# A planned kernel re-planned: new priorities and costs, VectorE and GpSimd kept apart in the plan, 30 unread matmuls behind the last output

## The chip, the cores and the metric

One core of a Trainium2 chip runs the whole problem. The metric is the device time in microseconds (us) of one execution; three executions of the kernel before gave 342.11, 342.50 and 342.98 us, median 342.5 us.

## The reference, cut to what matters

The problem is an attention block with quadratic features, followed by a gated feed-forward block with a spatial gate. Batch 4, 4 heads, sequence 1088, head width 32, model width 128, feed-forward width 1024.

```python
def phi(x):                       # 8 x 8 products of two projections of each row
    a = einsum('rd,bhsd->bhsr', S1, x); b = einsum('rd,bhsd->bhsr', S2, x)
    return einsum('bhsi,bhsj->bhsij', a, b).reshape(..., 64)
q_p, k_p = phi(q), phi(k)
kv, z = einsum('bhsf,bhsd->bhfd', k_p, v), sum(k_p, axis=2)
x = (q_p @ kv) / (q_p @ z + 1e-6)            # heads side by side: [4, 1088, 128]

h = gelu_tanh(x @ w_in)                      # [4, 1088, 1024]
u, v = h[..., :512], h[..., 512:]
v_n = (v - mean(v)) / sqrt(var(v) + 1e-6) * g_ln
v_s = einsum('ts,bsd->btd', w_sg, v_n) + b_sg[None, :, None]   # 1088 x 1088 along the sequence
out = x + (u * v_s) @ w_out
```

The product with `w_sg` (1088 by 1088, for each of 4 batches and 512 channels) is most of the arithmetic.

## The kernel before, in words

TensorE holds a float32 number as a sum of two float32r words (`_h` and `_l`), and a product of two such numbers is three float32r matmuls: high by high, low by high, high by low. VectorE and ScalarE make the words: ScalarE copies a tile into float32r (the high word), VectorE subtracts it from the tile (the low word). A few small products (features of k, sums over k, a transposition, the last output) stay in float32, and each of their matmuls stands as two instructions in the trace.

The sequence is cut into nine tiles of 128 rows, the outputs of the spatial product into three column blocks `CH` of 362, 362 and 364. Batch 0 runs first: attention (functions ending in `_0`), then the normalised gate tiles, then the spatial product, in which lines 744, 746 and 748 are the three kinds of matmul of `z0` and lines 1248, 1250 and 1252 those of the next block of channels. The matrix `w_sg` comes in as float32, ScalarE makes its high words (`w_h`, line 717), and GpSimd makes most of its low words (`w_l`, line 761, function `w_lo`, 21 pieces); the last two tiles go to VectorE (`late_low`, line 768). The words of a gate tile are made at lines 722 and 723 (function `part`). For batches 1 to 3 a scheme with fewer products runs (function `pair`), which needs combinations of `w_sg` that `combine` makes (lines 945 to 955) and sends through DRAM. While one batch runs, `attention(b)` prepares the next (lines 983 and 991 are its k products, 1010 the low words of q, 1031 and 1033 its feature products, 1073 to 1075 the gate half of the first layer).

Nothing in the text of the program sets the order of the work. Each step is a task given to `Plan.add` with its engine, a duration that the author supplies, the keys it reads and writes, and the buffers it takes and frees. `Plan.order` then plays all engines forward: it gives each TensorE task a due time from its position `pos`, works due times back through the dependencies, and at every moment picks the task that can start first, the earlier due time ahead. The resulting sequence is written out engine by engine, so that each engine runs its instructions in exactly this order, and one that waits holds up all behind it. Positions come from tables (`HEAD`, `SIDE`, `UNITS`, `OUTS`). The supplied durations are functions of the column count:

```python
dv = lambda n: 0.075 + n * 1.04e-3     # VectorE
ac = lambda n: 0.09 + n * 0.83e-3      # ScalarE
pe = lambda n: 0.005 + n * 0.443e-3    # TensorE
```

In this plan VectorE and GpSimd never hold one another up. A piece of `w_lo` is planned at 0.92 us, and the seven steps of `split64` (the float64 weights turned into float32, lines 512 to 518) at 0.42 to 0.67 us each for 512 columns.

At the start 14 matmuls whose result nobody reads run on TensorE (line 315). At the end, `finish` (lines 1185 to 1195) makes the last output block in two halves: two VectorE steps, float32 matmuls of 182 columns (line 1191), an addition on VectorE, and one DMA for each half, on SyncE's and on ScalarE's queue.

Of the kernel before, what the change touches and what calls it, by code (L numbers as in the profile page):

```python
# [18 lines left out]
P = 128  # L19
# [22 lines left out]
HEAD = [  # L42
# [5 lines left out]
]  # L48
SIDE = [
    dict(  # L50
        k=[-66.1568, -83.0896, -64.9264, -188.0582, -81.0397, -187.723, -70.4624, -77.7272, -77.1695],
        m=[-5466.7093, -5528.8972, -5437.2895, -5515.3945, -5393.6818, -5437.3893, -5432.8724, -5431.1056, -5501.4403],
        q=[634.6912, 673.1882, 647.6791],
        n=[64.1725, 20.8317, 52.3833, 22.0789, 61.9314, 20.9482],
        v=[11.3231, 63.8001, 41.2931, 152.8686, 24.7648, 29.2218, 100.774, 74.9017, 33.0816],
    ),
    dict(
        k=[104.6639, 64.2414, 66.2022, 93.2106, 94.9278, 59.1733, 77.7462, 87.1414, 48.0262],
        m=[68.9081, 117.0063, 70.3394, 41.7758, 72.8224, 116.9436, 126.4316, 41.681, 63.3969],
        q=[852.2799, 861.6072, 861.644],  # L60
        n=[161.3675, 69.9811, 170.238, 131.9103, 210.1209, 170.0751],
        v=[254.1817, 359.0423, 298.7528, 265.5773, 271.6818, 346.4955, 246.9949, 378.9035, 373.6698],
    ),
    dict(
        k=[445.2317, 1445.0667, 347.8146, 1453.4091, 1437.2462, 338.8656, 338.4801, 305.2576, 1462.8265],
        m=[240.7848, 278.0785, 215.5893, 305.508, 281.8525, 193.6687, 261.5745, 239.3695, 222.0321],
        q=[50.5261, 76.0513, 90.6998],
        n=[9375.8047, 9362.4456, 9374.739, 9361.4134, 9375.5758, 9369.7237],
        v=[127.1668, 148.5901, 276.214, 166.0724, 146.6282, 183.2742, 285.7286, 189.6866, 298.3922],
    ),  # L70
]
UNITS = [
    [41.9793, 27.5684, 38.7608],
    [147.9841, 100.1362, 157.0333],
    [169.7846, 137.9183, 129.767],
    [-33.9611, -31.7642, 487.2107],
    [631.6264, 620.4938, 639.6873],
    [1176.1661, 1190.4829, 1174.4149],
    [1286.0986, 1285.4686, 1259.311],
    [1120.4627, 1088.6707, 1101.0447],  # L80
    [174.8899, 174.1921, 174.7564],
    [53.0992, 83.7767, 45.9969],
    [176.2013, 188.4403, 182.9185],
    [151.0717, 161.8047, 172.948],
    [2273.7069, 2316.3133, 2263.2321],
    [5199.6257, 5107.2826, 5108.796],
    [40.0875, 25.0253, 23.3802],
    [1191.973, 1191.1916, 1192.4143],
]
OUTS = [  # L90
    [-0.3445, 11.4454, -11.4747],
    [202.992, 203.0658, 205.4131],
    [-9.1239, -4.2989, 47.4457],
    [638.4281, 736.5059, 730.313],
    [432.0253, 382.0212, 436.7813],
    [-22.0562, -0.7362, -25.8101],
    [565.5554, 575.2591, 561.2372],
    [-23.4218, 22.1653, -28.2736],
    [-23.1409, -8.8413, 1.757],
    [69.2499, -36.941, -43.6304],  # L100
    [3.6224, 443.7439, 439.3914],
    [1520.0977, 1533.1464, 1521.1808],
    [2020.1792, 1998.4613, 2022.0916],
    [-33.5198, -32.7719, -44.5421],
    [217.0347, 211.7791, 208.6139],
    [-45.2017, -46.2515, 4.5],
]
# [18 lines left out]
class Plan:  # L126
# [5 lines left out]
    def __init__(self, units):  # L132
        self.tasks, self.units, self.got = [], units, {}
        self.wrote, self.read = {}, {}

    def add(self, eng, dur, f, r=(), w=(), take=(), free=(), pos=None, late=None, start=None, after=(), kb=0):
        n = len(self.tasks)
        take = dict(take)
# [14 lines left out]
        self.tasks.append(dict(eng=eng, dur=dur, f=f, deps=deps, take=take, free=list(free), pos=pos, late=late, start=start, kb=kb))  # L153
# [6 lines left out]
    def order(self, free, t0):  # L160
# [20 lines left out]
        self.got, seq = {}, []  # L181
        clock = dict(free)
# [25 lines left out]
        while len(seq) < total:  # L208
            for e in stale:
                best[e] = None  # L210
                for i in can[e]:
                    x = max(clock[e], ready[i])
                    for k in T[i]["take"].values():
                        if not units[k]:
                            break
                        x = max(x, units[k][0][0])
                    else:
                        if best[e] is None or (x, last[i], i) < best[e]:
                            best[e] = x, last[i], i
# [11 lines left out]
            clock[e] = x + T[i]["dur"]  # L231
            if e == "SP" and T[i]["kb"]:
# [19 lines left out]
def tile_kernel(ctx: ExitStack, tc: tile.TileContext, qd, kd, vd, sd, wd, bd, wind, gd, woutd, identd, outd):  # L252
# [153 lines left out]
    pe = lambda n: 0.005 + n * 0.443e-3  # L406
# [33 lines left out]
    turns = iter(HEAD)  # L440

    def step(name, eng, dur, f, after=(), **kw):
        if eng == "PE":
            kw["pos"] = next(turns)
# [54 lines left out]
    def split64(name, hi, lo, raw, n, whole, after, last, by=V):  # L499
# [28 lines left out]
        step((name, "hi"), "A", 0.62, lambda: A.copy(hi, t()), [(name, 3)])  # L528
        step((name, "l1"), "V", 1.0, lambda: V.tensor_sub(t(), t(), f32(hi)), [(name, "hi"), (name, 5)])
        step((name, "l2"), "G" if by is G else "V", d[8] * 2.0, lambda: by.tensor_add(lo, t(), e()), [(name, "l1"), (name, 6)], w=last)  # L530
# [63 lines left out]
    for c in range(3):  # L594
        pk = ("pk0", c)
        step(pk, "PE", 0.68, lambda c=c: k1_0(c), ["sk", "k0" if c == 0 else "k1"], take={pk: "ps"})
        step(("kb0", c), "A", 0.25, lambda c=c: A.copy(kb0(c), ps(("pk0", c))[:, : 3 * P].rearrange("p (t c) -> p t c", t=3)[:, :, 32:64]), [pk])
        for i in range(3):
            t = 3 * c + i
            kk = [("vn", 2, t, x) for x in range(2)]  # L600
            step(("kp0", t), "V", 0.4, lambda c=c, i=i, t=t: features(vn[:, t, 512:768], ps(("pk0", c))[:, P * i : P * i + P], kb0(c)[:, i]),
# [43 lines left out]
    step("sabl", "G", 1.37, lambda: G.tensor_sub(sw[1], sab().rearrange("q x p c -> q (x p c)"), f32(sw[0])), ["sabh"])  # L645
# [702 lines left out]
```

## Time and profile before

| | us |
|---|---|
| median of three runs | 342.5 (342.11 to 342.98) |
| profiled execution, span from first to last instruction | 340.6 |
| the median less this span (what lies around the span) | 1.9 |
| TensorE busy | 327.8 (96%) |
| VectorE busy | 268.3 (79%) |
| ScalarE busy | 220.5 (65%) |
| GpSimd busy | 51.5 (15%) |

The profiled execution is told by its span; no other time of it is given, so the median stands beside it. A row of a timeline gives the start and the length of an instruction; matmuls are pipelined, so the distance of two starts is the time that one costs, and the length is about twice that. The bracket at the end of a timeline row is the idle time of the engine ahead of it, and who ended it. The 40 slices of the page are 8.5 us each.

### The profile page before, as it was taken

How to read it: one execution, taken by the hardware profiler on the slowest of the kernel's cores; microseconds unless marked ns; L12 is line 12 of the kernel's file. 1: busy time of each engine (PE TensorE's matmuls, PEld its weight loads, DVE VectorE, ACT ScalarE, POOL GpSimd, SP SyncE). 2: the span in 40 equal slices, each digit the busy share in tenths (PEclk: the TensorE clock that was granted, in tenths of full speed). 3: DMA queues.
4: the chain of work that ended last, by engine and by line, in shares of the span. 5: the costliest groups of instructions: out<-in, count | busy, mean ns of one | idle time of the engine just before them, and what ended most of it. 6: DMA issues, size and time to landing. Idle time of an engine off the chain costs nothing.

```text
span 340.6 us, 6042 instructions
## 1 busy us (share of the span) xinstructions
PE 327.8 (96%) x1988; PEld 319.1 (94%) x1988; DVE 268.3 (79%) x603; ACT 220.5 (65%) x533; POOL 51.5 (15%) x123
## 2 busy tenths in 40 slices
PE   8989869998999999999999999999999999999995
PEld 8987769998999989999998999999999999999994
DVE  4888999978976599999965699879854985786663
ACT  6689851376889975845669985487589834343330
POOL 1795681000003200000000600000021200000000
PEclk9999997999999999999999999999999999999999
DMA  7999174547746767999888356694569737384711
GB/s 241 371 398 334 36 201 120 133 114 195 186 146 192 197 184 229 276 275 312 265 262 246 111 167 206 177 311 146 174 179 283 241 102 247 104 269 117 237 41 65
DMA packets 56175, 68.87 MB, mean 202 GB/s; under 512 B 5008, under 2 KB 53456, under 8 KB 56144
## 3 DMA queue, kind: packets, MB, share of 16 engines
q1 hardware_dynamic: 56000, 68.40, 66.3%
q8 instruction: 15, 0.25, 0.3%
q14 instruction: 16, 0.13, 0.1%
q10 hardware_dynamic: 144, 0.09, 0.1%
HBM read 59.48 MB, written 8.99 MB: 201 GB/s over the span
## 4 chain that ended last, share of the span: by engine, by line
PE 83%; DVE 7%; DMA 6%; issue 1%; ACT 1%; SPq 0%; DVEq 0%
PE pz L892 15%; PE pz L894 15%; PE pz L893 15%; PE ps L807 2%; PE po L846 2%; PE ps L809 2%; PE ps L808 2%; PE po L845 2%; PE po L844 2%; PE ps L991 2%; PE pz L903 2%; PE pz L904 2%; DMA eb<-dq 2%; PE ps L1073 2%; PE ps L1075 2%; PE ps L1074 2%
## 5 line engine op out<-in xcount | busy, mean ns | idle before, releaser
L892 PE MATMUL pz<-w_h,ar 128*128 128x362 f32 (+1 forms) x288 | 96.1, 334 | 0.0
L894 PE MATMUL pz<-w_l,ar 128*128 128x362 f32 (+1 forms) x288 | 94.5, 328 | 0.0
L893 PE MATMUL pz<-w_h,ar 128*128 128x362 f32 (+1 forms) x288 | 94.3, 328 | 0.0
L892 PEld LDWEIGHTS pz<-w_h,ar 128*128 128x128 f32 x288 | 54.3, 188 | 0.5
L893 PEld LDWEIGHTS pz<-w_h,ar 128*128 128x128 f32 x288 | 54.3, 188 | 0.5
L894 PEld LDWEIGHTS pz<-w_l,ar 128*128 128x128 f32 x288 | 54.2, 188 | 0.0
L867 ACT CAST ar<-vn 128x512 fp32r<-128x512 f32 x40 | 24.5, 618 | 25.9 <-PE pz L894 25.1
L868 DVE TENSOR_TENSOR ar<-vn,ar 128x512 fp32r<-128x512 f32 x40 | 27.4, 686 | 13.4 <-ACT ar L867 13.0
L366 POOL TENSOR_TENSOR st<-st 128x4 f32<-128x4 f32 (+2 forms) x8 | 2.3, 285 | 189.5 <-DVE st L348 189.5
L838 ACT CAST gh<-gt 128x362 fp32r<-128x362 f32 (+1 forms) x47 | 23.0, 493 | 10.1 <-PE po L845 7.2
L813 ACT ACTIVATE u<-ps 128x362 f32<-128x362 f32 (+1 forms) x48 | 22.3, 471 | 10.9 <-DVE gt L837 6.5
L839 DVE TENSOR_TENSOR gl<-gt,gh 128x362 fp32r<-128x362 f32 (+1 forms) x47 | 24.7, 530 | 4.4 <-ACT gh L838 3.3
L383 ACT ACTIVATE vn<-vn,st 128x512 f32<-128x512 f32 x33 | 25.5, 811 | 0.6 <-POOL st L377 0.6
L837 DVE TENSOR_TENSOR gt<-gt,u 128x362 f32<-128x362 f32 (+1 forms) x47 | 24.6, 529 | 0.5 <-ACT u L813 0.2
L761 POOL TENSOR_TENSOR w_l<-w_f,w_h 128x362 fp32r<-128x362 f32 (+1 forms) x21 | 22.8, 1110 | 2.4 <-ACT w_h L717 2.1
L823 DVE SCALAR_TENSOR_TENSOR gt<-pz,g_col,b_bc 128x362 f32<-128x362 f32 (+1 forms) x31 | 18.1, 592 | 4.8 <-PE pz L894 3.4
L1085 ACT ACTIVATE kp<-vn,st 128x512 bf16<-128x512 f32 x27 | 19.5, 722 | 0.3
L1082 ACT ACTIVATE vn<-ps 128x512 f32<-128x512 f32 x27 | 16.0, 593 | 4.9 <-PE ps L1075 4.8
L991 PE MATMUL ps<-vx,kp 128*128 128x128 f32 x108 | 15.9, 275 | 0.7 <-DVE kp L320 0.7
L846 PE MATMUL po<-gl,wout_h 128*128 128x362 f32 (+1 forms) x47 | 15.6, 332 | 0.9 <-DVE gl L839 0.9
L807 PE MATMUL ps<-x_h,win_h 128*128 128x362 f32 (+1 forms) x48 | 16.0, 333 | 0.0
L809 PE MATMUL ps<-x_l,win_h 128*128 128x362 f32 (+1 forms) x48 | 15.8, 328 | 0.0
(298 smaller groups left out, 808.5 us busy)
## 6 DMA issues: line engine op xcount, KB each, us to landing
w_l<-td SPq DMA_DIRECT2D x96, 181.0 KB, 4.8
w_h<-td SPq DMA_DIRECT2D x48, 362.0 KB, 4.0
w_f<-in_w SPq DMA_DIRECT2D x9, 544.0 KB, 8.7
tmp<-in_w SPq DMA_DIRECT2D x16, 181.0 KB, 3.2
vx<-in_v SPq DMA_DIRECT2D x8, 288.0 KB, 4.1
ea<-dq SPq DMA_DIRECT2D x12, 182.0 KB
eb<-dq SPq DMA_DIRECT2D x12, 182.0 KB, 5.4
td<-tmp SPq DMA_DIRECT2D x8, 271.5 KB, 3.9
```

What stands on the lines that cost most here:

```text
L383: A.activation(self.vn(t), self.vn(t), AF.Identity, bias=self.nm[:, t : t + 1], scale=self.rs[:, t : t + 1])
L761: G.tensor_sub(w_l[t][:, cs], w_f[t][:, cs], f32(w_h[:, t, cs]))
L807: mm(o, lhsT=win_h[:, ws], rhs=xh[:, cs], start=True, stop=False)
L837: add("V", dv(cw), lambda: V.tensor_mul(gt(k)[:, :cw], gt(k)[:, :cw], utt[plan.got[u]][:, :cw]), r=[u], w=[k], free=[u])
L838: add("A", ac(cw), lambda: A.copy(ght[plan.got[h]][:, :cw], gt(k)[:, :cw]), r=[k], take={h: "gh"})
L839: add("V", dv(cw), lambda: V.tensor_sub(glt[plan.got[l]][:, :cw], gt(k)[:, :cw], f32(ght[plan.got[h]][:, :cw])), r=[h, k], take={l: "gl"}, ...
L867: add("A", ac(n), lambda: A.copy(dst[:, 0], q()), r=r, w=[key])
L868: add("V", dv(n), lambda: V.tensor_sub(dst[:, 1], q(), f32(dst[:, 0])), r=r, w=[key])
L892: mm(o, lhsT=ar[e][:, 0, t], rhs=wh, start=first, stop=False, skip_group_check=True)
L893: mm(o, lhsT=ar[e][:, 1, t], rhs=wh, start=False, stop=False, skip_group_check=True)
L894: mm(o, lhsT=ar[e][:, 0, t], rhs=wl, start=False, stop=last, skip_group_check=True)
L991: mm(ps(pkv)[:, P * p : P * p + P], lhsT=kpt[t % 3][:, P * p : P * p + P], rhs=vx[:, NT : NT + t + 2 : t + 1] if p else vx[:, t : NT + 1 : ...
```

## The change

The position tables go. Each TensorE task that had an entry in a table gets an offset from a list `OFF` of 269 numbers instead, and 1,320 of the tasks, on all engines, get a number from a table `BIAS` that is added to their due time. The supplied durations are changed, many of them downward (`split64` 0.35 and 0.61 us; gate statistics 0.81 for 0.87; ScalarE reading PSUM 0.058 us fixed for 0.09). Tasks can carry `port=1`: such a task on VectorE and such a task on GpSimd are planned one after the other, never side by side. The mark stands on the low words of the gate tiles (723), of the areas (`words`), of the gates (837 and 839), `split64`, `w_lo`, `late_low` and the two GpSimd subtractions of batch 0's attention. It does not stand on the low words of q (1010), on the steps of `combine` (945 to 955) or on the feature products (1031, 1033). No instruction's operands are changed and none is taken away; only the order is new. Behind the whole sequence come 30 matmuls on float32r operands, six widths five times each, into the three PSUM tiles `ps`, whose results nobody reads.

```diff
-HEAD = [ ... ]
-SIDE = [ ... ]
-UNITS = [ ... ]
-OUTS = [ ... ]
+OFF = [ ... ]
+BIAS = { ... }
...
-    def add(self, eng, dur, f, r=(), w=(), take=(), free=(), pos=None, late=None, start=None, after=(), kb=0):
+    def add(self, eng, dur, f, r=(), w=(), take=(), free=(), pos=None, late=None, start=None, after=(), kb=0, port=0, tune=None):
         n = len(self.tasks)
+        if tune is not None:
+            pos = (pos or 0.0) + OFF[len(self.tuned)]
+            self.tuned.append((n, tune))
...
             last[i] = x
+        for i, x in BIAS.items():
+            last[i] += x
...
                     x = max(clock[e], ready[i])
+                    if T[i]["port"]:
+                        x = max(x, port)
...
             clock[e] = x + T[i]["dur"]
+            if T[i]["port"]:
+                port = clock[e]
+                stale.update("VG")
...
-    pe = lambda n: 0.005 + n * 0.443e-3
+    pe = lambda n: 0.003 + n * 0.4487e-3
+    ap = lambda n: 0.058 + n * 0.83e-3
...
-        d = [0.13] * 9 if n == 16 else [0.46, 0.65, 0.42, 0.67, 0.42, 0.44, 0.67, 0.69, 0.69]
+        d = [0.15] * 9 if n == 16 else [0.35, 0.61, 0.35, 0.61, 0.35, 0.35, 0.61, 0.61, 0.69]
         for i, f in enumerate(ops):
-            step((name, i), "V", d[i], f, after)
+            step((name, i), "V", d[i], f, after, port=int(n > 16))
...
-        step((key, "l"), "V", dv(P * n), lambda: V.tensor_sub(ar[e][:, 1, x], q, f32(ar[e][:, 0, x])), w=[key])
+        step((key, "l"), "V", dv(P * n), lambda: V.tensor_sub(ar[e][:, 1, x], q, f32(ar[e][:, 0, x])), w=[key], port=1)
...
-            lo = [add("G", 0.92, lambda t=t, c=c: w_lo(t, c), w=[("w", t, c, 1)], r=[("w", t, c, 0)], after=lo)]
+            lo = [add("G", 0.92, lambda t=t, c=c: w_lo(t, c), w=[("w", t, c, 1)], r=[("w", t, c, 0)], after=lo, port=1)]
...
     with tc.manual_schedule():
         for i in seq[cut:]:
             plan.tasks[i]["f"]()
+        for i, n in enumerate((64, 128, 192, 224, 256, 288)):
+            for j in range(5):
+                mm(pst[i % 3][:, :n], lhsT=w_h[:, j, :P], rhs=w_h[:, j, P : P + n], start=True, stop=True)
```

## Rows read from the trace of the kernel before

**Rows 1.** Page, part 1: busy time, share, instructions.

```profile
PE 327.8 (96%) x1988; PEld 319.1 (94%) x1988; DVE 268.3 (79%) x603; ACT 220.5 (65%) x533; POOL 51.5 (15%) x123
```

**Rows 2.** Waits of PE: waiter, releaser, us in total, times, longest.

```profile
PE po L748 <- DVE ar L723: 2.8, 1, 2.8
PE ps L983 <- ACT vn L699: 1.4, 2, 0.9
PE pz L622 <- DVE vn L669: 1.0, 1, 1.0
...
PE po L846 <- DVE gl L839: 0.9, 1, 0.9
PE ps L991 <- DVE kp L320: 0.7, 1, 0.7
PE ps L983 <- DVE kp L320: 0.7, 1, 0.7
```

**Rows 3.** Timeline of PE at 51 us: start, length, instruction, idle before.

```profile
51.00 0.43 PE L748 MATMUL po<-w_h,ar 128*128 128x362 f32 x1 [2.83 <-DVE ar L723]
```

**Rows 4.** Windows: us, busy of each engine (instructions), PE clock, DMA share, GB/s.

```profile
48.00:51.00 3.00, 0.17 (x3) 0.01 (x1) 3.00 (x6) 1.12 (x3) 2.06 (x2) 1.00 0.57 186
...
51.40:54.70 3.30, 3.30 (x13) 3.30 (x12) 3.27 (x6) 0.66 (x3) 0.00 (x0) 0.50 0.29 84
```

**Rows 5.** Timeline of DVE, 42 to 51 us.

```profile
43.08 1.30 DVE L1010 TENSOR_TENSOR qtl<-qld,qth 128x364 fp32r<-128x364 f32 x1
44.30 1.11 DVE L954 TENSOR_TENSOR tmp<-tmp 128x181 fp32r<-128x181 f32 x1
...
46.71 1.45 DVE L723 TENSOR_TENSOR ar<-vn,ar 128x512 fp32r<-128x512 f32 x1
48.08 1.17 DVE L514 TENSOR_SCALAR sp_wi_m<-sg_wraw_wi 128x512 int32<-128x512 int32 x1
...
50.53 0.41 DVE L723 TENSOR_TENSOR ar<-vn,ar 128x256 fp32r<-128x256 f32 x1
```

**Rows 6.** Timeline of POOL in the same stretch.

```profile
42.92 7.14 POOL L761 TENSOR_TENSOR w_l<-w_f,w_h 128x362 fp32r<-128x362 f32 x6
```

**Rows 7.** Timeline of DVE from 115 us on, POOL idle.

```profile
115.74 0.54 DVE L1010 TENSOR_TENSOR qtl<-qld,qth 128x364 fp32r<-128x364 f32 x1 [1.38 <-ACT qth L1009]
...
119.39 0.35 DVE L946 TENSOR_TENSOR tmp<-tmp 128x181 f32<-128x181 f32 x1 [1.30 <-DMA tmp<-in_w]
...
121.28 0.34 DVE L954 TENSOR_TENSOR tmp<-tmp 128x181 fp32r<-128x181 f32 x1
```

**Rows 8.** Timeline of DVE, 14 to 18 us.

```profile
14.15 0.42 DVE L516 TENSOR_SCALAR sp_wi_e<-sg_wraw_wi 128x512 int32<-128x512 int32 x1
14.49 1.20 DVE L517 TENSOR_SCALAR sp_wi_g<-sp_wi_t 128x512 int32<-128x512 int32 x1
```

**Rows 9.** Windows of ACT's full stretch and of VectorE's fullest later one.

```profile
33.00:37.00 4.00, 1.84 (x12) 1.30 (x11) 3.54 (x12) 4.00 (x17) 2.27 (x7) 1.00 0.38 127
...
140.00:160.00 20.00, 20.00 (x122) 19.85 (x121) 19.77 (x42) 11.96 (x27) 0.00 (x0) 1.00 0.95 284
```

**Rows 10.** Timeline of PE at the end, matmuls of 364 columns.

```profile
332.25 0.33 PE L892 MATMUL pz<-w_h,ar 128*128 128x364 f32 x1
...
332.75 0.33 PE L892 MATMUL pz<-w_h,ar 128*128 128x364 f32 x1
```

**Rows 11.** Chain that ended last, in order of time: start, us, what.

```profile
22.34 2.63 PE pz L622 x24
...
120.62 0.89 PE ps L991 x8
...
336.34 0.59 PE po L1191 x2
```

**Rows 12.** Timeline and DMA view: last issue; issues with KB and us to landing.

```profile
337.59 0.37 ACTq L1195 DMA_DIRECT2D out<-gt  x1
...
out<-gt SPq DMA_DIRECT2D x8, 181.0 KB, 1.8
```

More of the change, by code (lines that the diff above doesn't have):

```diff
@@ L72 @@
[L72 to L107, printed above, removed]
+OFF = [
[17 rows of a table added]
+]
@@ L110, in f32 @@
+BIAS = {
[110 rows of a table added]
+}
 def f32(ap):
@@ L152, in add @@
         late = (2.3 + kb / 300 if eng == "SP" else self.LATE.get(eng, 0)) if late is None else late
-        self.tasks.append(dict(eng=eng, dur=dur, f=f, deps=deps, take=take, free=list(free), pos=pos, late=late, start=start, kb=kb))
+        self.tasks.append(dict(eng=eng, dur=dur, f=f, deps=deps, take=take, free=list(free), pos=pos, late=late, start=start, kb=kb, port=port))
         return n
@@ L181, in order @@
         self.got, seq = {}, []
+        port = 0.0
         clock = dict(free)
@@ L439, in tile_kernel @@
     ids = {}
-    turns = iter(HEAD)
     def step(name, eng, dur, f, after=(), **kw):
         if eng == "PE":
-            kw["pos"] = next(turns)
+            kw["tune"] = name
         ids[name] = add(eng, dur, f, after=[ids[a] for a in after], **kw)
@@ L527, in split64 @@
             return
-        step((name, "hi"), "A", 0.62, lambda: A.copy(hi, t()), [(name, 3)])
-        step((name, "l1"), "V", 1.0, lambda: V.tensor_sub(t(), t(), f32(hi)), [(name, "hi"), (name, 5)])
-        step((name, "l2"), "G" if by is G else "V", d[8] * 2.0, lambda: by.tensor_add(lo, t(), e()), [(name, "l1"), (name, 6)], w=last)
+        step((name, "hi"), "A", 0.52, lambda: A.copy(hi, t()), [(name, 3)])
+        step((name, "l1"), "V", 0.61 if n > 16 else 0.15, lambda: V.tensor_sub(t(), t(), f32(hi)), [(name, "hi"), (name, 5)], port=1)
+        step((name, "l2"), "G" if by is G else "V", 1.38 if by is G else d[7] - 0.08, lambda: by.tensor_add(lo, t(), e()), [(name, "l1"), (name, 6)], w=last, port=1)
     prev = []
@@ L595, in tile_kernel @@
         pk = ("pk0", c)
-        step(pk, "PE", 0.68, lambda c=c: k1_0(c), ["sk", "k0" if c == 0 else "k1"], take={pk: "ps"})
-        step(("kb0", c), "A", 0.25, lambda c=c: A.copy(kb0(c), ps(("pk0", c))[:, : 3 * P].rearrange("p (t c) -> p t c", t=3)[:, :, 32:64]), [pk])
+        step(pk, "PE", 1.3 if c < 2 else 0.8, lambda c=c: k1_0(c), ["sk", "k0" if c == 0 else "k1"], take={pk: "ps"})
+        step(("kb0", c), "A", 0.14, lambda c=c: A.copy(kb0(c), ps(("pk0", c))[:, : 3 * P].rearrange("p (t c) -> p t c", t=3)[:, :, 32:64]), [pk])
         for i in range(3):
@@ L727, in last_part @@
         step((("rs", i), "h"), "A", 0.23, lambda: A.copy(rs[:, i], q), [("v3", NT - 1)], w=[("rs", i)])
-        step((("rs", i), "l"), "V", 0.23, lambda: V.tensor_sub(rs[64:, i], q[64:], f32(rs[64:, i])), w=[("rs", i)])
+        step((("rs", i), "l"), "V", 0.23, lambda: V.tensor_sub(rs[64:, i], q[64:], f32(rs[64:, i])), w=[("rs", i)], port=1)
     for t0 in range(0, 8, 2):
@@ L772, in tile_kernel @@
         if t >= LOWS:
-            lo = [add("V", 1.25 + 0.6 * (t == NT - 1), lambda t=t: late_low(t), w=[("w", t, c, 1) for c in range(3)], r=[("w", t, c, 0) for c in range(3)], after=lo)]
+            lo = [add("V", 1.2 + 1.0 * (t == NT - 1), lambda t=t: late_low(t), w=[("w", t, c, 1) for c in range(3)], r=[("w", t, c, 0) for c in range(3)], after=lo, port=1)]
             continue
@@ L809, in f @@
             mm(o, lhsT=win_h[:, ws], rhs=xl[:, cs], start=False, stop=True)
-        pemain(3 * pe(cw), f, UNITS[4 * b + db][ci], r=[("win",)] + [("x", b % 2, c) for c in range(3)], take={k: "ps"})
+        pemain(3 * pe(cw), f, ("pu", b, db, ci), r=[("win",)] + [("x", b % 2, c) for c in range(3)], take={k: "ps"})
         u = ("u", b, q)
-        add("A", 0.05 + ac(cw), lambda: A.activation(utt[plan.got[u]][:, :cw], ps(k)[:, :cw], AF.Gelu_apprx_tanh),
+        add("A", 0.02 + ap(cw), lambda: A.activation(utt[plan.got[u]][:, :cw], ps(k)[:, :cw], AF.Gelu_apprx_tanh),
             r=[k], take={u: "u"}, free=[k], after=gone(b))
@@ L836, in gate @@
         k, u, h, l = ("gt", b, q), ("u", b, q), ("gh", b, q), ("gl", b, q)
-        add("V", dv(cw), lambda: V.tensor_mul(gt(k)[:, :cw], gt(k)[:, :cw], utt[plan.got[u]][:, :cw]), r=[u], w=[k], free=[u])
+        add("V", dv(cw), lambda: V.tensor_mul(gt(k)[:, :cw], gt(k)[:, :cw], utt[plan.got[u]][:, :cw]), r=[u], w=[k], free=[u], port=1)
         add("A", ac(cw), lambda: A.copy(ght[plan.got[h]][:, :cw], gt(k)[:, :cw]), r=[k], take={h: "gh"})
-        add("V", dv(cw), lambda: V.tensor_sub(glt[plan.got[l]][:, :cw], gt(k)[:, :cw], f32(ght[plan.got[h]][:, :cw])), r=[h, k], take={l: "gl"}, free=[k])
+        add("V", dv(cw), lambda: V.tensor_sub(glt[plan.got[l]][:, :cw], gt(k)[:, :cw], f32(ght[plan.got[h]][:, :cw])), r=[h, k], take={l: "gl"}, free=[k], port=1)
         i = nout[b, ci] = nout.get((b, ci), 0) + 1
@@ L867, in words @@
         add("A", ac(n), lambda: A.copy(dst[:, 0], q()), r=r, w=[key])
-        add("V", dv(n), lambda: V.tensor_sub(dst[:, 1], q(), f32(dst[:, 0])), r=r, w=[key])
+        add("V", dv(n), lambda: V.tensor_sub(dst[:, 1], q(), f32(dst[:, 0])), r=r, w=[key], port=1)
     def split(b, db, half, e):
@@ L976, in attention @@
             load_("", 300, lambda p=p: vd_(p), w=[("vx", p)])
-        side = SIDE
-        pkv = ("pkv", b)
+            pkv = ("pkv", b)
         for t in range(NT):
@@ L1077, in attention @@
             need = sorted({min(2, P * t // 364), min(2, (P * t + P - 1) // 364)})
-            add("PE", 3 * pe(DG), v1, r=[("x", b % 2, c) for c in need], take={pv: "ps"}, pos=at(b, "v", t))
+            add("PE", 3 * pe(DG), v1, r=[("x", b % 2, c) for c in need], take={pv: "ps"}, tune=at(b, "v", t))
             pair = lambda x: x.rearrange("p (s d) -> p s d", s=2) if b % 2 else x
@@ L1215, in at @@
     def at(b, kind, i):
-        return SIDE[b - 1][kind][i]
+        return (kind, b, i)
     def standard(b, db, ci, zi, e, i):
```

86 lines of the change are left out of this document (31 added, 55 removed), and 132 rows, old and new, of tables (BIAS, HEAD, OFF).

## The prediction, made before the changed kernel ran

> **What bounds the kernel now.** The page's busy line comes first: TensorE is busy for 327.8 of 340.6 us [rows 1], so a new order can give back only TensorE's idle time and the time in which its clock is low; it takes no matmul away. The waits of TensorE, read next, say where the idle time is: one wait of 2.8 us on the VectorE tile `ar`, and six more of 0.7 to 1.0 us [rows 2]. The timeline and the windows then say what they are worth. The 2.83 us stand ahead of the matmul at 51.00 us [rows 3]; VectorE is busy for all of 48 to 51 us, and directly after the gap TensorE's clock is at 0.50, the 1.2 GHz level, for 51.4 to 54.7 us, in which thirteen matmuls run [rows 4]. In the gap itself TensorE was busy for only 0.17 of 3 us [rows 4].
>
> Why VectorE was late stands in its own timeline. In the stretch before, GpSimd runs six pieces of `w_lo` back to back, 7.14 us from 42.92 us on [rows 6], and VectorE's instructions are stretched beside them: the low words of q 1.30 us and a step of `combine` 1.11 us [rows 5], where the same lines take 0.54 and 0.34 us with GpSimd idle [rows 7]; a low-word step of 512 columns 1.45 us and a `split64` step 1.17 us [rows 5]. The piece of `ar` that TensorE waits for starts only at 50.53 us, behind all of them, and takes 0.41 us itself [rows 5]. The old plan's supplied durations know none of this: it took 0.42 us for the step that took 1.17.
>
> **What the change takes away.** The plan now puts marked VectorE and GpSimd tasks one after the other, so it sees that VectorE is short here and can put the `ar` pieces ahead of work that is not due. I count the wait of 2.83 us as gone [rows 3], and with it the slow clock behind it: 3.3 us at half rate lose 3.3 x 0.5 = 1.65 us [rows 4]. What is late next is the same engine. The mark is missing on the low words of q and on `combine`, and these were stretched by 1.30 - 0.54 = 0.76 and 1.11 - 0.34 = 0.77 us [rows 5, 7], so the plan is still up to 1.53 us too optimistic where it puts them beside `w_lo`; I leave half of it, 0.8 us, as a wait.
>
> The same stretching delays batch 0's attention. A `split64` step of 0.42 us is followed by one of the same kind and width of 1.20 us [rows 8], and TensorE then waits 1.0 us for the product behind it [rows 2]. I count that wait as gone. The two waits on ScalarE (1.4 us together) and the first of the two on `kp` (0.7 us) lie in 33 to 37 us, where ScalarE is busy for 4.00 of 4 us [rows 2, 9]: no order makes that engine shorter, and I give nothing, with 0 and 2.1 us as the ends. The 0.7 us on the second `kp` [rows 2] stand behind a VectorE step at 119.39 us that had itself waited 1.30 us for a DMA [rows 7], and I take the 0.9 us on `gl` [rows 2] to be alike; how the plan forecasts a landing is unchanged, so such waits can come again anywhere: nothing again, with 1.6 us as the most. Below nothing, a plan that is new everywhere can open a wait where the old one had none; its price is a rival's, below. Gain of the order: 2.83 + 1.65 - 0.8 + 1.0 = 4.7 us; the ends are 4.7 + 0.8 + 2.1 + 1.6 = 9.2 and, with one new wait of the old one's size and its slow clock, 4.7 - 4.5 = 0.2 us.
>
> The shorter supplied durations move no time of themselves, since an engine takes what it takes; what they change is the order, counted above. The moved DMA issues are covered likewise: SyncE's queue only issues, and its lateness would show as waits of the kind just bounded.
>
> On the lock itself the rows show lengths, not a mechanism. The Trainium skill, "SBUF — State Buffer", section "SBUF: two separate sides", says that VectorE and GpSimd share a port pair under an exclusive lock, taken by VectorE for two SBUF inputs or a two-port mode and held for the whole instruction, and that the loser is blocked entirely. By that rule the unmarked steps block as fully as the marked ones, which speaks against the change being a complete cure; without the rule the 0.8 us would be a guess between 0 and 1.53 all the same, so the sum stands.
>
> **What the change adds.** Thirty matmuls, 5 x (64 + 128 + 192 + 224 + 256 + 288) = 5,760 columns, are queued on TensorE behind the last one that counts. They delay no operand, but the program ends only when TensorE has ended too. Before, TensorE's last work begins at 336.34 and takes 0.59 us, to 336.93 [rows 11]; the last DMA is issued at 337.59 and an output DMA lands 1.8 us after its issue, so about 339.4 [rows 12], and the span ends 1.2 us later. So 339.4 - 336.93 = 2.5 us of added matmuls are covered by the last DMA, and each us beyond is a us of the span.
>
> No narrow float32r matmul is in the trace, so bounds. From below, by columns alone: three of 364 columns take 0.50 us [rows 10], 0.458 ns a column, so 2.64 us, 0.1 us beyond the cover. From above, as float32, where each matmul is two instructions: of 66 columns 24 take 2.63 us, of 128 columns 8 take 0.89 us [rows 11], 0.11 us each at either width; beyond 128 in proportion, 0.167, 0.194, 0.222 and 0.25 us. Two of each, five times: 5 x 2 x (0.11 + 0.11 + 0.167 + 0.194 + 0.222 + 0.25) = 10.5 us, 8 us beyond the cover. Between them: that 66 columns cost as much as 128 says that an instruction with a full stationary tile has a floor of 0.11 us. I take one instruction a matmul, as every float32r matmul of the trace is, at the larger of floor and columns: 5 x (4 x 0.11 + 0.117 + 0.132) = 3.45 us, 0.9 us beyond the cover.
>
> The Trainium skill, "TensorE: Matmul & The Clock Gate", section "LDWEIGHTS (loading the stationary operand)", puts a weight load at its columns over 1.2 GHz, 107 ns for 128; by that, as an estimate, the 30 take 3.4 us. It bears out the floor as a weight load's, and the rows above give the same without it.
>
> **Sum.** 340.6 - 4.7 + 0.9 = 336.8 us of span; with the 1.9 us by which the median lies above the profiled span, 338.7 us.
>
> **Rivals.**
> Narrow float32r costs what float32 does. By the nearest width, 64 to 224 columns are nearer to the float32 rows of 66, 128 and 182, and 256 and 288 to float32r at 364: 5 x (2 x (0.11 + 0.11 + 0.167 + 0.194) + 0.117 + 0.132) = 7.1 us, 4.6 beyond the cover, so the gain is used up: 342.5 - 4.7 + 4.6 = 342.4 us. For it: no float32r row is narrower than 360 columns. Against: nothing in the rows makes float32r depend on width.
> The slower side: all six widths at the float32 price, 10.5 us at the very end, 342.5 - 4.7 + 8.0 = 345.8 us. It decides from 2.5 + 4.7 = 7.2 us of added matmuls on; from there the kernel is slower whatever the order brought. Against it: the 364-column rows, close to 288, show one instruction at one pass.
> The order gives nothing: one new wait as long as the old one, with its slow clock, in a stretch where VectorE has no slack, as 140 to 160 us with 19.77 of 20 busy [rows 9]. Its price is 2.83 + 1.65 = 4.5 us: 343.2 us, and more if there are two. For it: there TensorE has no gap now, so any swap can only lose. Against: GpSimd is idle there, and the durations without it are what the plan supplies.
> The order gives more: the waits on ScalarE and on landed DMAs shrink too, and the matmuls stay under the cover: 342.5 - 8 + 0.5 = 335 us.
>
> **How the numbers follow.** Forecast, 336.5 to 341 us: 46%. Nearest width: 24%, with the order's gain uncertain by some 3 us so 5 faster, 13 the same, 6 slower. All float32: 7%, slower. The order gives nothing: 15%, 8 the same, 7 slower. The order gives more: 8%. A change under 0.3%, 1 us, can't be told from none here. Faster 46 + 5 + 8 = 59%, same 21%, slower 20%. The range of 335.3 to 344.0 leaves out the all-float32 case, the worse half of the nothing case, a few of the nearest-width case and the best of the better one, just under 2 in 10.
>
> **What would show it.** Right: no TensorE wait over 1.5 us after 20 us, no window behind 10 us at clock 0.5, shorter VectorE steps beside `w_lo` around 42 to 51 us or the same ones with `ar` ahead; at the end 30 matmuls whose starts lie 0.11 us apart up to 224 columns and follow the columns above. Wrong in the tail: start distances that fall sharply between 224 and 256 columns, or two instructions a matmul. Wrong in the order: a wait of TensorE on VectorE of 2 us or more anywhere, or a last real matmul that ends later than 334 us.

## The result: slower by 5.5 us, and the profile after

The changed kernel takes 348.25 us (median of 4 runs, 346.36 to 348.82) where the kernel before takes 342.74 (4 runs beside them, 342.11 to 345.25): a ratio of 1.0134, interval 1.0091 to 1.0178 (the ratio is not the quotient of the medians; by it the loss is 4.6 us). The forecast was 338.7 us with a range to 344.0; both the sign and the range were wrong. The two profiled executions differ by 6.4 us of span, 347.0 for 340.6.

Lines of the changed kernel are about 76 higher than the same lines before: `ar` of batch 0 is 799 for 723, its product 824 for 748, `w_lo` 837 for 761, the gate product 968 to 970 for 892 to 894, `gt` 899 for 823, the low words of q 1085 for 1010. The busy line of the page first; it answers to [rows 1]:

```profile
PE 335.9 (97%) x2018; PEld 320.7 (92%) x2018; DVE 265.2 (76%) x603; ACT 219.6 (63%) x533; POOL 52.7 (15%) x123
```

TensorE is busy for 8.1 us more. The 30 matmuls are 3.8 of them; the rest is no added work. The busy line can't say where a loss is: a matmul behind a gap is drawn longer (one of 364 columns at 0.41 us below, 0.33 in [rows 10]), and short gaps between matmuls are drawn as busy. The waits of TensorE (waiter, releaser, us in total, times, longest) answer to [rows 2]:

```profile
PE po L824 <- DVE ar L799: 2.3, 3, 1.0
PE pz L968 <- DVE gt L899: 1.5, 2, 1.2
PE pz L656 <- DVE vn L396: 1.5, 1, 1.5
...
PE pz L968 <- DMA w_h<-td: 0.6, 2, 0.4
```

The one wait of 2.83 us on `ar` has become three that sum to 2.3 us; those on ScalarE and `kp` at 33 to 37 us have shrunk to 0.3 and 0.2 us; new are waits on the late product (968) for a VectorE tile and for streamed weights. The share of the chain by engine says the same of the whole run; first the page of before, then that of after:

```profile
PE 83%; DVE 7%; DMA 6%; issue 1%; ACT 1%; SPq 0%; DVEq 0%
```

```profile
PE 65%; DVE 14%; DMA 12%; ACT 3%; issue 3%; POOL 2%; SPq 1%; POOLq 0%; DVEq 0%; ACTq 0%
```

To place the loss I add up, in both traces, the distance from each matmul's start to the next, less the median distance that the same source line and shape has in the trace of before. This "lost time" holds gaps and slow clock alike; how rows are grouped moves such a sum by up to 0.3 us:

| lost time, us | 0 to 120 us | behind 120 us | last matmul that counts starts at |
|---|---|---|---|
| before | 10.7 | 0.4 | 336.60 |
| after | 8.8 | 7.7 | 342.14 |

The new order gains 1.9 us up to 120 us and loses 7.3 us behind it, where the old order lost next to nothing. 7.3 - 1.9 = 5.4, and the last matmul that counts starts 5.5 us later.

**The tail.** TensorE's timeline at the end (start, length, instruction) shows the 30 matmuls one behind the other, and the view of that tile gives their first and last start:

```profile
341.19 1.27 PE L1266 MATMUL po<-gt,kp 128*128 128x182 f32 x4
342.17 3.77 PE L1389 MATMUL ps<-w_h 128*128 128x64 f32 x30
```

```profile
L1389 PE MATMUL ps<-w_h x30: 272/278/319, 342.2 to 345.6; 128*128 128x64 f32 x5, 128*128 128x128 f32 x5, 128*128 128x192 f32 x5, 128*128 128x224 f32 x5
```

One instruction a matmul, some 3.5 us from first to last start and one more distance to the end of the last, 3.6 in all. The first distance of each width is longer, 0.125 to 0.154 us; the others are on average 0.111 to 0.112 us at 64, 128, 192 and 224 columns, 0.118 at 256 and 0.130 at 288. The prediction had 0.11, 0.117 and 0.132, and 3.45 us in all. From the last output DMA's issue to the end of the span it is 2.97 us before and 3.90 after: by this reading the tail costs 0.93 us, for a predicted 0.9.

**Behind 120 us.** The windows (us, busy of each engine with its instructions, clock, DMA share, GB/s) of after and of before; the stretch of 140 to 160 us before is in [rows 9], with TensorE at 20.00:

```profile
140.00:160.00 20.00, 18.78 (x112) 18.20 (x111) 17.63 (x37) 10.20 (x21) 0.00 (x0) 1.00 0.97 294
...
220.00:240.00 20.00, 19.32 (x112) 18.24 (x111) 16.98 (x37) 11.11 (x23) 0.00 (x0) 1.00 1.00 285
```

```profile
220.00:240.00 20.00, 20.00 (x118) 19.61 (x118) 15.28 (x31) 14.41 (x36) 0.00 (x0) 1.00 0.76 224
```

The clock is full in all of them, so the loss of this execution is gaps. In 220 to 240 us the DMA engines are busy for all of the stretch where before they had a quarter free; in 140 to 160 us they were as full before (0.95 in [rows 9]), and TensorE lost nothing there. The chain (start, us, what) through the largest gap:

```profile
143.28 0.56 SPq L1103
143.89 5.93 DMA eb<-dq
149.91 0.92 DVE ea L1106
150.83 0.60 DVE ar L944
151.43 0.45 DVE r L1132
151.88 0.83 DVE eb L1108
152.71 0.45 DVE x_l L1135
153.15 0.52 DVE gt L899
153.80 0.41 PE pz L968
```

A fill of `eb` goes out as two transfers, the first issued at 143.28 us; the second takes 5.93 us to land. VectorE runs in written order, so its next instruction (1106) holds up all behind it: the row of its timeline has 1.54 us of idle ahead, and `gt`, which TensorE needs, comes fifth behind it. TensorE's row has 1.22 us.

```profile
149.91 0.92 DVE L1106 TENSOR_TENSOR ea<-ea,eb 128x728 f32<-128x728 f32 x1 [1.54 <-DMA eb<-dq]
```

```profile
153.80 0.41 PE L968 MATMUL pz<-w_h,ar 128*128 128x364 f32 x1 [1.22 <-DVE gt L899]
```

In the old order the same fill, the fifth of nine, left 10 us: issued at 136.76, used at 146.78. In the new one VectorE was ready 5.1 us after the issue (149.91 - 1.54 - 143.28). Over all nine the old order left 4.7 to 10.0 us (median 7.1) and VectorE waited at one, 1.3 us; the new one left 4.6 to 11.5 (median 5.5) and VectorE waited at four, 0.7 to 1.9 us, the longest of which the view puts down to another transfer, `out<-gt`. The distance alone does not decide: two fills of the old order left 4.9 and 4.7 us and held up nothing, where the trace has landings of 4.3 and 2.9 us. The two rows of before, SyncE's queue and VectorE:

```profile
136.76 1.20 SPq L1028 DMA_DIRECT2D eb<-dq  x2
```

```profile
146.78 0.91 DVE L1031 TENSOR_TENSOR ea<-ea,eb 128x728 f32<-128x728 f32 x1
```

The gaps at 183 and 224 us have the same start (a fill of 6.50 us, a weight load of 5.74 us). The one at 284 us has another: GpSimd's normalisation of a batch. The one at 194 us has both: its chain runs from the fill of 6.50 us to a normalisation of 3.6 us from 188.03 us on. The timeline of GpSimd ahead of the gap at 284 us:

```profile
273.80 0.57 POOL L442 TENSOR_TENSOR st<-st 128x4 f32<-128x4 f32 x1 [9.20 <-DVE st L424]
274.45 0.37 POOL L443 TENSOR_TENSOR st<-st 128x4 f32<-128x4 f32 x1
274.91 0.51 POOL L444 TENSOR_SCALAR st<-st 128x4 f32<-128x4 f32 x1
...
277.44 0.20 POOL L449 TENSOR_TENSOR st<-st 128x4 f32<-128x4 f32 x1
```

Instructions that take 0.20 us with VectorE idle take 0.37 to 0.57 beside it, on four columns; the eleven took 4.7 us. (Before, one such chain from 262.34 us on took 4.1, and TensorE waited for nothing behind it.) Behind them stand four `vn` steps on ScalarE, the words of `ar`, and TensorE.

**Up to 120 us.** The rows that answer to [rows 5, 6]: VectorE, GpSimd and TensorE of after between 42 and 52 us.

```profile
43.55 1.00 DVE L799 TENSOR_TENSOR ar<-vn,ar 128x256 fp32r<-128x256 f32 x1
...
44.81 0.96 DVE L1085 TENSOR_TENSOR qtl<-qld,qth 128x364 fp32r<-128x364 f32 x1
45.69 1.11 DVE L1030 TENSOR_TENSOR tmp<-tmp 128x181 fp32r<-128x181 f32 x1
...
47.06 0.87 DVE L799 TENSOR_TENSOR ar<-vn,ar 128x256 fp32r<-128x256 f32 x1
47.85 1.18 DVE L1078 TENSOR_TENSOR kvl<-kp,kvh 128x256 fp32r<-128x256 f32 x1
```

```profile
43.31 6.55 POOL L837 TENSOR_TENSOR w_l<-w_f,w_h 128x362 fp32r<-128x362 f32 x6
```

```profile
51.59 0.43 PE L824 MATMUL po<-w_h,ar 128*128 128x362 f32 x1 [1.04 <-DVE ar L799]
```

Six pieces of `w_lo` run back to back as before, and VectorE works beside them all the while. Marked tasks too: the `ar` pieces of 256 columns take 1.00 and 0.87 us, for 0.41 in [rows 5], and a `split64` step behind them 1.19, for 0.41 to 0.43 alone. The exclusion is in the plan's forecast only; what is written out is an order for each engine, and no wait of one for the other goes with it. In this execution the slow clock is still there, in another place: 0.50 at 35.2 to 38.6 us, behind a stretch in which TensorE was busy for 0.34 of 1 us (for 51.4 to 54.7 us in [rows 4]).

```profile
34.00:35.00 1.00, 0.34 (x2) 0.27 (x2) 0.90 (x6) 1.00 (x4) 0.00 (x0) 1.00 0.36 119
35.20:38.60 3.40, 3.40 (x13) 3.40 (x12) 3.19 (x11) 1.58 (x7) 2.64 (x9) 0.50 0.23 60
```

Other executions show what of this belongs to the order. In the traces of after_no_tail, after_thin and after_quick (below), whose order is the same up to here, the waits on `ar` are 2.9 us in three, the longest 1.7, and there is no slow clock in 30 to 60 us; in that of before_tail, whose order is the old one, a wait of 2.6 us on `ar` stands as before, with the clock at 0.50 behind it and at 36.2 us as well. So the wait on `ar` came back in pieces in each of these traces of the new order, and where the slow clock falls changes from one execution to the next.

### The profile page after: what moved, and what is told of

It is laid out like the page before. It is cut to its first block, busy times and chain, and to the rows that moved or that the text cites. A ratio compares the mean times of both kernels' runs of the same rounds, so it can differ in the third digit from the quotient of the medians.

```text
span 347.0 us, 6080 instructions
## 1 busy us (share of the span) xinstructions
PE 335.9 (97%) x2018; PEld 320.7 (92%) x2018; DVE 265.2 (76%) x603; ACT 219.6 (63%) x533; POOL 52.7 (15%) x123
## 4 chain that ended last, share of the span: by engine, by line
PE 65%; DVE 14%; DMA 12%; ACT 3%; issue 3%; POOL 2%; SPq 1%; POOLq 0%; DVEq 0%; ACTq 0%
PE pz L968 12%; PE pz L969 11%; PE pz L970 11%; DMA eb<-dq 5%; DMA w_h<-td 3%; PE ps L1066 2%; PE ps L883 2%; PE ps L1148 2%; PE po L922 2%; PE pz L980 2%; PE pz L979 2%; PE ps L885 2%; PE ps L884 2%; PE po L920 2%; PE po L921 2%
## 5 line engine op out<-in xcount | busy, mean ns | idle before, releaser
L396 DVE TENSOR_TENSOR kp<-ps,kb 128x256 f32<-128x256 f32 x27 | 11.1, 417 | 6.6 <-ACT kb L1061 3.9
```

## The experiments

One execution of a kernel lies up to 1% from the next (before: 341.06 to 344.54 us in 23 runs), so medians of many runs carry the verdicts, and single profiles only say where.

### Where the loss is

`after_no_tail` is the changed kernel without its last lines:

```diff
-        for i, n in enumerate((64, 128, 192, 224, 256, 288)):
-            for j in range(5):
-                mm(pst[i % 3][:, :n], lhsT=w_h[:, j, :P], rhs=w_h[:, j, P : P + n], start=True, stop=True)
```

> The changed kernel without its 30 unread matmuls; its order is untouched. Theory A (the order lost the time, the added matmuls cost only what reaches past the last output's DMA): 0.9 us less than the changed kernel, 347.3 us. Rival B (the added matmuls are what made it slower): back to the kernel before, 342.7 us or less.

Measured: 348.27 us in four runs, ratio 1.0146 [1.0091, 1.0201]. The tail is not the loss. The trace is a second look at the new order, and its largest gap is not the one above: a streamed weight, issued at 140.67 us in the chain, takes 6.25 us to land, TensorE waits 2.00 us, and behind that its clock is at 0.50 for 3.4 us.

```profile
146.96 0.64 PE L970 MATMUL pz<-w_l,ar 128*128 128x362 f32 x1 [2.00 <-DMA w_l<-td]
```

```profile
147.00:150.40 3.40, 3.40 (x11) 3.40 (x12) 2.24 (x7) 1.13 (x2) 0.00 (x0) 0.50 0.95 274
```

The tail's 0.9 us lie inside the spread; `before_tail`, which puts the 30 matmuls behind the old order, has the same limit:

> The kernel before, its order untouched, with the 30 unread matmuls behind the last output. If they cost what the span's end showed (0.93 us beyond the cover of the last DMA), 343.4 to 343.7 us, a ratio of 1.0027; if they cost more than the span's end can show, over 344.5 us; if the last DMA covers them whole, 342.7 us.

Measured: 342.42 us for 342.39, ratio 1.0005 [0.9979, 1.0031]. Over 344.5 us is ruled out, 0.9 us (0.27%) is not told from nothing. In its profile the last DMA's issue lies 3.77 us ahead of the end of the span, 0.80 us more than before. The tail's cost rests on these readings of the span's end, not on the times.

Four kernels take the new order up to a point of the plan and the old one behind it, or the other way round; the tasks and their code are the same in all. The edit, cut to its main line, with a remark of this text:

```diff
-        while len(seq) < total:
+        for i in SEQ:    # new_then_old: new order to 128 us of its plan, then the old; _58, _92: to 58, 92 us
```

> The new order up to the task planned at 128 us, from there on the remaining tasks in the order of the kernel before; no added matmuls. Theory A (the new order is 1.9 us better up to 120 us and 7.3 us worse behind, and the two parts are independent): 342.7 - 1.9 = 340.8 us. Rival C (the early order sets up the late waits, or the old late order only works behind the old early one): 345 us or more.

> The order before up to the task planned at 128 us, from there on the remaining tasks in the new order; no added matmuls. Theory A: 342.7 + 7.3 = 350 us. Rival C (the late waits come from the early order): about 343 us.

> The new order only up to what is planned at 58 us, the old one behind it, without the 30 matmuls. The loss after 120 us should be gone as in new_then_old. If the new order gains the 1.9 us that its trace shows up to 120 us already before 58 us, and the junction there costs nothing, 340.5 to 341.2 us; if what a cured wait gives back comes up as other waits behind it, as in before_ar_first, 342.2 to 342.9 us.

> The new order up to what is planned at 92 us, the old one behind it, without the 30 matmuls. Same two theories: 340.5 to 341.2 us if the early gain is real and lies before 92 us; 342.2 to 342.9 us, as with the junction at 128 us, if it is given back.

| kernel | median, us | ratio | lost to 120 us | lost behind |
|---|---|---|---|---|
| new_then_old | 342.72 | 0.9986 [0.996, 1.0013] | 9.3 | 2.5 |
| old_then_new | 351.78 | 1.0264 [1.0205, 1.0322] | 9.5 | 10.5 |
| new_then_old_58 | 342.35 | 1.0009 [0.9979, 1.0039] | 12.7 | 1.6 |
| new_then_old_92 | 346.68 | 1.0128 [1.0085, 1.017] | 14.4 | 0.6 |

The late half of the new order is slow behind either early half, and the late half of the old order is not. The junctions cost something of their own: 4 us at 92 us (lost time 6.4 us in 80 to 120 us), where neither theory had expected a loss; 4 of the 10.5 us of old_then_new lie in 120 to 140 us; and new_then_old loses 2.1 us behind 120 us that the old order does not. So its time, that of before and not the 340.8 us of theory A, doesn't say that the early half gains nothing. Two readings say that it gains a little. Of the traces in the three tables whose first 120 us are all of one order, the six with the new one lose 8.0 to 9.8 us there, the four with the old one 9.5 to 10.7. And the granted clock, as a mean over the span, is 0.998 on average over the 12 runs of new_then_old and 0.992 over the 23 of before beside them: 0.006 of 340 us, by estimate 2 us. No kernel with the new early half alone turns this into time. The lost times are of one execution each, and that of new_then_old_58 is the longest of its twelve (345.45 us).

### Why the early gain did not come

`before_ar_first` is the old order with the late `ar` piece alone moved: ahead of five tasks, four of them VectorE's.

```diff
 VectorE's order from 45 us on, in words (ScalarE's step 1002, which waits for 999, goes behind its step 1019)
 split64 (513)
+ar, 256 columns (723)
 ar, 512 columns (723)
 split64 (514)
 kp (999)
 split64 (515)
-ar, 256 columns (723)
```

> The kernel before with one change in VectorE's order: the ar piece that TensorE waited 2.83 us for is put ahead of four VectorE instructions (a 512-column ar piece, two split64 steps and the masked kv). Theory D (the prediction's first step: that wait and the slow clock behind it were worth 4.5 us and nothing else was late): 338.2 us, and no window at clock 0.5 behind 10 us. Rival E (VectorE is the bound of this stretch, so the next piece is late in its place): between 340.5 and 342.7 us, with a new wait of TensorE on VectorE before 60 us.

Measured: 342.85 us for 342.73, ratio 1.0001 [0.9964, 1.0039]. The wait of 2.83 us is gone from its trace, and lost time in 40 to 60 us falls from 3.3 to 1.0 us. But the slow clock comes at 37.2 us instead of 51.3, and stretches that had little loss get some: 1.6 us more in 60 to 100 us and 1.5 in 140 to 180. A slow clock at 36 us is in the trace of before_tail too, without any swap, so that part may be chance. Theory D, 338.2 us, is out by the interval. That the time which VectorE lacks is owed to whatever stands next fits the rows, but is read from one trace.

`before_lo_one` leaves the old order alone and takes away the stretching: GpSimd's `w_lo` reads one SBUF operand, the subtraction is left out, and the instruction is of another kind.

```diff
-        G.tensor_sub(w_l[t][:, cs], w_f[t][:, cs], f32(w_h[:, t, cs]))
+        G.tensor_scalar(w_l[t][:, cs], w_f[t][:, cs], 1.0, None, op0=ALU.mult)
```

> The kernel before, its order untouched, with GpSimd's low words of the gate matrix made by an operation that reads one SBUF operand instead of two (the low words then hold w_f itself, so the subtraction is left out). Theory J, the stretching beside GpSimd comes with two SBUF operands on both engines: VectorE's low words of q at 43 us fall from 1.30 to near 0.54 us, the step of combine from 1.11 to near 0.34, the 2.83 us wait on the low words of the attention areas goes, TensorE's lost time of 40 to 60 us falls from 3.27 to about 1, and the median by 1 to 3 us, to 339.7 to 341.7. Theory K, GpSimd beside VectorE stretches it whatever it reads: lengths and wait stay within 20 per cent, and the time at 342.4 to 342.8 us.

Measured: 340.94 us for 343.07, ratio 0.9942 [0.9913, 0.9971]: theory J, by its middle. VectorE's and GpSimd's rows of its trace:

```profile
44.31 0.52 DVE L1010 TENSOR_TENSOR qtl<-qld,qth 128x364 fp32r<-128x364 f32 x1
44.76 0.62 DVE L954 TENSOR_TENSOR tmp<-tmp 128x181 fp32r<-128x181 f32 x1
...
45.91 0.68 DVE L723 TENSOR_TENSOR ar<-vn,ar 128x512 fp32r<-128x512 f32 x1
...
49.92 0.74 DVE L517 TENSOR_SCALAR sp_wi_g<-sp_wi_t 128x512 int32<-128x512 int32 x1
```

```profile
42.26 8.12 POOL L761 TENSOR_SCALAR w_l<-w_f 128x362 fp32r<-128x362 f32 x6
```

The low words of q take 0.52 us for 1.30, `combine` 0.62 for 1.11, `ar` 0.68 for 1.45 [rows 5], beside a GpSimd that is busy for longer (8.12 us for 7.14 [rows 6]). The wait on `ar` is not in its list. So most of the stretching goes when GpSimd reads one SBUF operand instead of two (or with the kind of its instruction; both changed). It does not need two operands on VectorE, as theory J had it: a `split64` step that reads one took 1.17 us beside the old `w_lo` [rows 5]. A rest stays, 0.62 us for `combine` for 0.34 alone, and 0.74 us for a `split64` step that takes 0.43 alone. The Trainium skill, "SBUF — State Buffer", section "SBUF: two separate sides", has a VectorE operation with two SBUF inputs and any GpSimd operation that reads SBUF lock each other out for a whole instruction; the 0.52 us beside a GpSimd that still reads SBUF don't agree, and the measurement decides. And 2.0 us (0.58% of 343; 1.0 to 3.0 by the interval) is what that stretching costs the old order, wait and all.

`after_lo_one` makes the same edit in the changed kernel without its tail.

> The changed kernel without the 30 matmuls, with GpSimd's low words of the gate matrix made by an operation that reads one SBUF operand (the subtraction is left out, the low words hold w_f). Beside GpSimd nothing is then stretched as before, so what the exclusion in the plan was to avoid is nearly gone. Theory L, the new order had already avoided most of the stretching: 347 to 348.5 us, under 1.3 us to be had. Theory M, VectorE lost as much to it as in the old order, only on other instructions: 345 to 346.8 us, the 2 us that the old order got, with its waits on the low words of the attention areas (2.9 us in three without the 30 matmuls) under 1 us. The late loss stays in both.

Measured: 345.08 us for 343.20, ratio 1.0061 [1.0032, 1.0091]; after_no_tail stood at 1.0146, so 0.85%, 2.9 us less (0.8 to 5.1 by the two intervals): theory M. The new order still paid for the stretching; whether more or less than the old one, the intervals don't say. Its waits on `ar` fall from 2.9 us in three to 1.0 in two, in a trace that is the shortest of its twelve executions.

### Why it is late behind 120 us

`after_thin` (no tail) has all 144 loads of the streamed weights bring 46 of 362 columns; `before_thin` does the same to the kernel before. The edit, without the like line for `w_h`:

```diff
-                load(f32(w_l[half + t][:, 362:724]), TD[n][t, 1])
+                load(f32(w_l[half + t][:, 362:408]), TD[n][t, 1][:, :46])
```

> The changed kernel without its 30 matmuls, and with thin stream loads: each of the 144 loads of combined w_sg words brings 46 columns instead of 362 (the other columns keep older values), in the same places of the same queue. Theory F (the late waits of TensorE come from DMAs that land later than the plan thinks, because stream loads share the DMA engines with the feature loads ea and eb): the waits at 140 to 155, 182 and 226 us go, about 4.5 of 7.5 us, 343.8 us; those behind a GpSimd normalisation (193 and 283 us) stay. Rival G (VectorE's and ScalarE's supplied durations are too short, DMAs are covered): 347 us or more, the waits stay.

> The kernel before with the same thin stream loads (46 of 362 columns). Theory F: its late part has no waits to lose, only a wait or two around 80 to 120 us that DMAs cause: 0 to 1 us less, 341.7 to 342.7 us, so that most of the distance to the changed kernel is gone. Rival G: 342.7 us, the distance stays at 4 to 5 us.

`after_quick` (no tail) and `before_quick` make GpSimd's normalisation of batches 1 to 3 of two instructions instead of eleven, which leaves out the rest of the square root, and `after_thin_quick` has both edits.

```diff
+            if self.b:
+                G.tensor_scalar(self.rs[:, ts], y, 1.875, None, op0=ALU.mult)
+                G.tensor_mul(self.nm[:, ts], self.mv[:, ts, 0], self.rs[:, ts])
+                return
```

> The changed kernel without its 30 matmuls, and with GpSimd's normalisation of batches 1 to 3 cut from eleven small operations to two (the Newton steps are left out). Theory H (the small GpSimd operations take 4.5 us instead of the planned 3.0, since they are not marked and VectorE stretches them, and this makes the waits at 193 and 283 us): 1.5 us less than the changed kernel, 346.7 us, and no TensorE wait at those places. Rival: ScalarE's queue is what is late there, nothing changes, 348.2 us.

> The kernel before, its order untouched, with GpSimd's normalisation of batches 1 to 3 in two operations instead of eleven (the rest of the square root is left out). If the old order already hides this normalisation, as its trace without late waits says, 342.0 to 342.9 us, and the 4.0 us that the same cut gave the new order are that order's own loss; if any order pays for it, 339 to 340 us.

> Both cuts at once: thin stream loads and the short normalisation, no added matmuls. Theories F and H together: the late part is as free of waits as that of the kernel before, 348.2 - 4.5 - 1.5 = 342.2 us. If only one of them holds, 343.8 or 346.7 us; if neither, 348 us.

| kernel | median, us | ratio to before | lost to 120 us | lost behind |
|---|---|---|---|---|
| after_no_tail | 348.27 | 1.0146 [1.0091, 1.0201] | 9.8 | 8.6 |
| after_thin | 342.91 | 1.0001 [0.997, 1.0031] | 8.0 | 3.0 |
| after_quick | 344.31 | 1.0029 [0.999, 1.0068] | 8.0 | 7.2 |
| after_thin_quick | 340.60 | 0.9922 [0.9887, 0.9957] | 8.5 | 1.0 |
| before_thin | 341.48 | 0.9966 [0.9934, 0.9999] | 9.5 | 0.3 |
| before_quick | 342.69 | 0.9982 [0.9953, 1.0011] | 9.7 | 1.0 |

By the ratios, of 342.7 us, thin loads take 5.0 us from the new order and 1.2 from the old, quick normalisation 4.0 from the new and 0.6 from the old (1.6 at the end of its interval); both together take 7.7 from the new. Each is more than was expected of it (343.8 and 346.7 us for 342.91 and 344.31). Beside after_thin, the quick normalisation takes 2.7 us more (1.1 to 4.3 by the intervals), beside after_quick the thin loads 3.7 (1.9 to 5.5), so neither stands in for the other. In after_thin TensorE has no gap left where the DMA engines had been full, first of these rows, and still loses where the normalisation stands, second:

```profile
140.00:160.00 20.00, 20.00 (x122) 19.94 (x121) 19.17 (x40) 11.93 (x24) 0.00 (x0) 1.00 0.42 90
...
260.00:280.00 20.00, 19.39 (x115) 18.68 (x114) 12.87 (x28) 15.42 (x34) 3.89 (x11) 1.00 0.09 14
```

In after_quick it is the other way: no loss in 280 to 300 us, and waits for streamed weights.

```profile
PE pz L972 <- DMA w_h<-td: 2.1, 3, 1.1
```

So the late loss has two causes, as theories F and H had it each for its part: DMA landings for which the new plan leaves too little, and a GpSimd chain for which it leaves what its durations say. That 5.0 + 4.0 is more than 7.7 is no finding, since each amount is uncertain by about 2 us; how the 7.7 us divide is open, and after_quick's profiled execution is the longest of its ten (346.25 us). Thin loads shorten the wait for a landing and free the DMA engines at once, and these two weren't told apart. No run gave the new order's fills their old distance back, so that the distance is at fault is read from the traces. Nor was it tried which part of the change, the priorities, the durations or the mark, took it away. The kernel before with both edits wasn't run either: by the sum of its two, 1.8 us, after_thin_quick would be 0.9 us ahead of it, which the intervals don't tell from nothing.

## Why the prediction was wrong, step by step

- **What bounds the kernel** stood: TensorE is the bound, and what an order changes is its gaps and its clock. The prediction read the gaps that were there. Behind 120 us there were none (0.4 us of lost time in 220 us), and in its sum the prediction gave that stretch nothing, without asking what kept it free.
- **"How the plan forecasts a landing is unchanged, so such waits can come again anywhere: nothing again, with 1.6 us as the most"** is the step that failed. Its 1.6 us are a gain; as a loss the sum had nothing, and the ends one new wait of 4.5 us. The forecast is unchanged, the distance behind it is not. The fifth fill had 10 us between its issue and its use, and then 5.1, with DMA engines at 0.97 to 1.00 of a stretch and landings of 5.7 to 6.5 us. This, with GpSimd's normalisation, which the prediction doesn't name, is 7.3 us of lost time where the sum had nothing; without both, the new order is at 0.9922 of the kernel before.
- **The wait of 2.83 us counted as gone, and with it the slow clock, 1.65**, failed for the most part. The wait became three, of 2.3 us together in the profiled execution and 2.9 in others. The slow clock is at 35 us in the profiled execution and absent there in others; over the runs it did shrink, by estimate 2 us. The early stretch gained 1.9 us in the profiled execution, for 4.7 predicted, and no time in the kernels that took only the early order. The prediction held that an order which knows of the stretching can put `ar` ahead of work that isn't due; before_ar_first did that in the old order and gained nothing that can be measured, and before_lo_one, which makes VectorE's work shorter, gained 2.0 us.
- **The 0.8 us left as a wait, for the unmarked steps**, was too small: the unmarked steps took 0.96 to 1.18 us again, and marked ones 0.87 to 1.19, since only the plan's forecast keeps them apart.
- **The wait of 1.0 us at 18 us as gone**: it is gone; TensorE has no wait in 10 to 30 us. But it is not in the traces of before_tail and before_quick either, whose early order is the old one, so this is no gain of the order. One of 1.5 us at 8.2 us (line 656) is no loss of it for the same reason: those two traces have 1.4 and 1.3 us at that place.
- **ScalarE and `kp`, nothing given**: here the new order did gain, 2.1 us of waits becoming 0.5.
- **The tail** was right in its step and its size: one instruction a matmul, floor 0.11 us to 224 columns, 3.45 us of work for 3.6, 0.9 us beyond the cover for 0.93. The 0.93 is read from the end of a span; the times are too coarse for it. The rivals of a float32 price fall.
- **The rival "the order gives nothing: one new wait"** was nearest to what happened, and named 140 to 160 us, where the largest gap came. Its price was one wait with its slow clock, 4.5 us. The profiled execution has many gaps at full clock instead, none over 1.3 us behind 120 us; in after_no_tail there is such a wait with its slow clock, 2.0 us at 147 us, but on a landing and not on VectorE. Of the signs that the prediction named, a wait over 1.5 us is in after_no_tail and not in the profiled execution, a window at clock 0.5 is in both, and the last real matmul is behind 334 us in both. The rival had the argument that should have carried more than 15%: where TensorE has no gap, a swap can only lose, and 220 of 340 us were such a stretch.

## What to carry to other kernels

Where a hand-tuned order is planned anew, price the stretches that have no wait now, not only the waits: list what each of them leans on (DMA issues and how long ahead of use they stand, chains on small engines) and ask whether the new plan's durations keep that distance. Planning two engines apart kept nothing apart here, since no wait went with it; ask which engine's work becomes shorter, because a swap alone may only choose who waits. Look at more than one execution before a single wait of 1 to 2 us, or one stretch of slow clock, is put down to an order. Where a long queue runs in order, the cost of a late landing is read at the instruction behind it that the bound engine needs.

## What the runs showed of the hardware

- A float32r matmul with a full stationary tile of 128 columns costs on average 0.111 to 0.112 us from start to start at 64 columns as at 224, then 0.118 at 256 and 0.130 at 288; the first distance of each width is 0.125 to 0.154.
- Beside a VectorE at work, GpSimd instructions on 128x4 elements take 0.37 to 0.57 us for 0.20; in a chain of eleven that is 4.7 us.
- Beside a GpSimd that reads two SBUF operands VectorE's low words of q take 0.96 to 1.30 us, beside one that reads one 0.52, near the 0.54 with GpSimd idle. A VectorE instruction that reads one operand takes 1.17 to 1.20 us beside the first, still 0.74 beside the second, and 0.43 alone.
- In one unchanged order the stretch of clock 0.50 stood at 51.3 us in one execution and at 36.2 and 53.3 us in another (before, before_tail).
